# Sparse chunk attention and a routed expert layer on one core: token layout by pairs of tiles, one PSUM bank per head, one gather row, later constants

## The chip, the cores and the metric

One core of a Trainium2 chip runs the whole program in one launch. The metric is device time in microseconds. Of the kernel before there are two runs, 395.28 and 399.24 us, median 397.26; a further execution was profiled. The engines are named as in the profile: PE (TensorE), PEld (its weight loads), DVE (VectorE), ACT (ScalarE), POOL (GpSimd) and SP (SyncE, which here only issues transfers).

## What is computed

Attention with 4 batches, 8 heads, 768 positions and 64 features. For each query an upper bound on its score with each chunk of 32 keys is formed from the chunk's smallest and largest key; the six best causal chunks are kept, and softmax attention runs over their causal keys alone. The result, as 3072 tokens of 512 features, goes through a dense layer pair for all tokens plus one of eight experts for each.

```python
k_min = np.min(k_chunks, axis=3); k_max = np.max(k_chunks, axis=3)
ub = sum(maximum(q * k_min, q * k_max), axis=-1)      # by query and chunk
ub = where(causal, ub, -1e9); top_chunks = argsort(ub)[..., -6:]
scores = scale * q @ k.T, kept where the chunk is in top_chunks and pos_q >= pos_k
attn = softmax(scores) @ v
x = attn.transpose(0, 2, 1, 3).reshape(3072, 512)
y = relu(x @ w1_dense) @ w2_dense
e = argmax(x @ w_gate);  gate = max(softmax(x @ w_gate))
y += gate * (relu(x @ w1[e]) @ w2[e])                  # each token's own expert
```

## The kernel before

**Attention** goes over 16 pairs of heads (`NP`), four to a batch. A tile is 128 consecutive tokens; a head has six (`NT`). For a pair p, `load` (L257) issues six transfers of 192 KB from SP, one for each of k, q, v and each head, in runs of one token's 64 floats (256 bytes). `cast` (L265) makes 16-bit copies on POOL. `prep_k` (L273) transposes k on PE, reduces it on DVE to chunk maxima and minima (L280, L281) and copies it to `kT` beside rows that carry the chunk mask (`exf`). `prep_q` (L288) transposes q, `prep_ub` (L298) forms the bounds by small products on top of the causal constant `cbias`, takes the eight largest of 24 by `max` (L311) and writes where a chunk is out (L313) into spare columns of `q16`; tile 0 is left out, since its queries see at most four chunks. `prep_s` (L316) transposes those columns with q, so one product gives masked scores.

The scores come in units of up to 512 columns (`PIECES`, L130): key tile bb against query tiles from bb on, 11 units a pair with both heads interleaved. `scores` (L324) is one or more products (L330), an exponential on ACT (L334) and, on the diagonal tile, a select on POOL (L344, `affine_select`) that clears later keys. `av` (L348) multiplies with v into `op`, one PSUM tile of two banks for both heads (L362), and `norm` (L366) divides at the end of the pair (L370, L371) into `xbig`.

The loop (L391) starts the scores two units ahead. At each pair's first unit it issues the loads of pair p + 3 (three load buffers), one expert weight on POOL (`load_expert`, 1 MB of floats, L126) and the casts of p + 2. After each batch the dense work of its tokens is queued as `fills`: transposes (L181), the gate (L189), two dense layers (L217, L226) and writes of x to `xd` (L206) and of the dense y to `yd` (L231). A planner of the framework orders each engine's instructions by its own cost estimates, so an instruction without dependences, such as a weight load, can stand earlier than in the text.

**Start.** Constants are made on POOL and DVE ahead of everything (L53 to L112); loads of pairs 0, 1 and 2, then `load_dense` and the casts follow.

**Routing** (L449 to L509): after the last batch's gate, token positions in expert-sorted blocks of 128 are computed on DVE and PE (31 blocks, `NBLK`); `gi` and `si` hold the gather and scatter rows.

**Expert blocks** (L590 on): `gather` fetches 128 rows of `xd` (1,056 bytes, L523) and 128 rows of `yd` (2,048 bytes, L526) from POOL's queue; `tx` transposes x (L533, copied at L535), `e1` is the first product (L541, ACT at L544), `th` transposes (L550, L552), `e2` the second (L558), the weighted sum `yo` with y on DVE (L561) and a scatter from POOL (L562). The tiles of x, y and yo have three buffers each (`eg`), and gathers run two blocks ahead.

## Time and profile before

| | |
|---|---|
| two runs, median | 397.26 us (395.28 to 399.24) |
| profiled execution | 394.51 us |
| its span, first to last instruction | 392.8 us |
| busy: PE, PEld | 258.8, 152.8 us |
| busy: DVE, ACT, POOL | 192.1, 159.7, 208.0 us |
| moved by DMA | 56.92 MB in 98,370 packets, of them 78,462 under 512 B |
| mean granted clock of PE | 0.907 of full |

Busy times overlap; a share over the whole span mixes three stages: attention to 213 us, routing to some 240 us, expert blocks to the end. In the slices each digit is the busy share in tenths of one fortieth of the span. A wait names who waited, for whom, and how long in all, how often, and the longest. Times in rows are microseconds from the start of the span; "mean ns" is one instruction's.

### The profile page before, as it was taken

The page shows a single profiled execution, that of the slowest core. Times are in us where ns is not written, and L with a number is a line of the kernel's source. Part 1 is how long each engine was busy: PE and PEld are TensorE (multiplying, and loading weights), DVE is VectorE, ACT ScalarE, POOL GpSimd, SP SyncE. Part 2 cuts the span into 40 slices and gives each one's busy share as a digit, 9 for nine tenths or more (in the row PEclk, how much of TensorE's full clock was granted, in tenths as well). Part 3 has the DMA queues.
Part 4 walks back from the last instruction along what each step waited for, and adds up shares of the span by engine and source line. Part 5 has one row for each costly group of instructions (what it writes and reads, how often), then busy time and mean ns, then how long its engine had stood idle before and what let it go on. Part 6 is the DMA issues. An engine that isn't in the chain of part 4 may idle for free. (4 is left out here: it accounts for less than half of the span.)

```text
span 392.8 us, 7052 instructions
## 1 busy us (share of the span) xinstructions
PE 258.8 (66%) x2426; PEld 152.8 (39%) x2426; DVE 192.1 (49%) x538; ACT 159.7 (41%) x303; POOL 208.0 (53%) x370
## 2 busy tenths in 40 slices
PE   0157377157599989999898872667555658565660
PEld 0135254045365666666665531333222323222230
DVE  8284438248387798777952890222222323232220
ACT  1016257056276867787675320322132222322230
POOL 9946185174455555554322025366756656666541
PEclk9998869779699999999999996888989996989895
DMA  9999999999997886211031425143444444444440
GB/s 182 208 222 214 208 204 198 170 199 204 222 236 191 190 200 145 94 53 56 3 119 49 164 106 173 42 154 114 131 133 132 149 145 135 134 136 133 128 121 0
DMA packets 98370, 56.92 MB, mean 145 GB/s; under 512 B 78462, under 2 KB 90750, under 8 KB 98336
## 3 DMA queue, kind: packets, MB, share of 16 engines
q1 hardware_dynamic: 81856, 28.42, 32.8%
q0 software_dynamic: 16480, 28.06, 30.1%
q8 instruction: 20, 0.33, 0.3%
q14 instruction: 14, 0.11, 0.1%
HBM read 50.08 MB, written 17.66 MB: 172 GB/s over the span
## 5 line engine op out<-in xcount | busy, mean ns | idle before, releaser
L334 ACT ACTIVATE ex<-sp 128x512 f16<-128x512 f32 (+1 forms) x176 | 91.7, 585 | 63.1 <-PE sp L330 31.1
L344 POOL TENSOR_SCALAR_AFFINE_SELECT ex<-ex 128x128 f16<-128x128 f16 (+1 forms) x176 | 52.2, 306 | 55.9 <-ACT ex L334 53.0
L362 PE MATMUL op<-v,ex 128*128 128x65 f16 x672 | 47.6, 200 | 34.6 <-POOL ex L344 29.7
L330 PE MATMUL sp<-r,kT 128*128 128x512 f16 (+3 forms) x256 | 65.1, 328 | 3.6 <-ACT ex L334 2.1
L362 PEld LDWEIGHTS <-ex 128*128 128x128 f16 x672 | 37.3, 101 | 49.5 <-POOL ex L344 35.0
L535 DVE COPY exT<-tp 128x512 f16<-128x512 f16 x31 | 13.2, 425 | 80.5 <-PE tp L533 59.3
L523 POOL DMA_INDIRECT xg<-xd,gi x31 | 30.3, 977 | 41.5 <-DVE yo L561 21.6
L552 ACT COPY ehT<-tp 128x512 f16<-128x512 f16 x31 | 18.2, 586 | 74.2 <-PE tp L550 67.9
L541 PE MATMUL hp<-we,exT 128*128 x124 | 37.4, 432 | 10.2 <-DVE exT L535 5.8
L558 PE MATMUL yp<-we,ehT 128*128 x124 | 38.8, 419 | 4.5 <-ACT ehT L552 2.6
L533 PE MATMUL tp<-ident,xg 128*128 128x128 f16 x124 | 14.2, 247 | 40.7 <-DMA xg<-xd,gi 40.7
L562 POOL DMA_INDIRECT out_dram<-yo,si x31 | 31.5, 1015 | 15.3 <-issue 13.4
L561 DVE SCALAR_TENSOR_TENSOR yo<-yp,xg,yg 128x512 f32<-128x512 f32 x31 | 23.3, 750 | 31.9 <-PE yp L558 27.2
L526 POOL DMA_INDIRECT yg<-yd,gi x31 | 29.4, 949 | 10.5 <-issue 10.2
L322 DVE COPY r<-pp 128x768 f16<-128x768 f16 x32 | 17.0, 554 | 32.8 <-PE pp L320 32.6
L544 ACT ACTIVATE eh<-hp 128x512 f16<-128x512 f32 x31 | 18.5, 597 | 35.2 <-PE hp L541 26.3
L533 PEld LDWEIGHTS <-xg 128*128 128x128 f16 x124 | 8.3, 108 | 56.9 <-DMA xg<-xd,gi 56.8
L217 PE MATMUL hp<-xT,wd 128*128 128x384 f16 x128 | 26.5, 325 | 0.7 <-ACT hT L219 0.3
L330 PEld LDWEIGHTS <-kT 128*128 128x128 f16 x256 | 21.8, 103 | 11.1 <-issue 8.2
L226 PE MATMUL yp<-wd,hT 128*128 128x512 f16 x96 | 24.6, 378 | 1.5 <-DVE xbig L371 1.0
L269 POOL CAST q<-qf 128x768 f16<-128x768 f32 x16 | 13.3, 831 | 21.5 <-DMA qf<-in_q_dram 20.9
L294 ACT ACTIVATE qp<-pp 128x768 f16<-128x768 f16 x16 | 13.0, 810 | 23.1 <-PE pp L292 23.1
(115 smaller groups left out, 431.0 us busy)
## 6 DMA issues: line engine op xcount, KB each, us to landing
we<-in_moe_w_dram POOLq DMA_DIRECT2D x16, 512.0 KB
kf<-in_k_dram SPq DMA_DIRECT2D x32, 192.0 KB, 4.4
qf<-in_q_dram SPq DMA_DIRECT2D x32, 192.0 KB, 4.5
vf<-in_v_dram SPq DMA_DIRECT2D x32, 192.0 KB, 4.7
yd<-ys SPq DMA_DIRECT2D x24, 256.0 KB, 2.1
xd<-xbig SPq DMA_DIRECT2D x4, 792.0 KB, 4.3
wd<-in_moe_w_dense_dram POOLq DMA_DIRECT2D x2, 512.0 KB
xg<-xd,gi POOLq DMA_INDIRECT x31
```

What stands on the lines that cost most here:

```text
L217: nc.tensor.matmul(hp, wd[:, ko, j * 128 : (j + 1) * 128], xT[:, ko, g * G * 128 : (g + 1) * G * 128], start=(ko == 0), stop=(ko == NK - 1))
L226: nc.tensor.matmul(yp, hold["h"][:, j, i * 128 : (i + 1) * 128], wd[:, NK + j], start=(j == 0), stop=(j == NK - 1))
L330: nc.tensor.matmul(sp[:, o : o + z - a], kT[p % NB][g][:, bb * 128 : (bb + 1) * 128], s["r", g][:, a:z], start=(o == 0), stop=True, skip_g ...
L334: nc.scalar.activation(ex[:, :o], sp[:, :o], AF.Exp, scale=0.125)
L344: nc.gpsimd.affine_select(out=exd, in_=exd, compare_op=ALU.is_ge, fill=0.0, base=0, pattern=[[0, n], [1, 128]], channel_multiplier=-1)
L362: nc.tensor.matmul(op[:, g, t * (D + 1) : (t + 1) * (D + 1)], ex[:, c : c + 128], v16[p % NB][:, g, bb, :], start=(u == g and n == 0), sto ...
L523: nc.gpsimd.indirect_dma_start(out=xg, out_offset=None, in_=xd, in_offset=bass.IndirectOffsetOnAxis(ap=gi[:, i : i + 1], axis=0))
L526: nc.gpsimd.indirect_dma_start(out=yg, out_offset=None, in_=yd, in_offset=bass.IndirectOffsetOnAxis(ap=gi[:, i : i + 1], axis=0))
L541: nc.tensor.matmul(hp, s["xT"][:, ko], wef[:, bass.ds(offs[i] + ko * 512, 512)], start=(ko == 0), stop=(ko == NK - 1))
L558: nc.tensor.matmul(yp, s["hT"][:, j], wef[:, bass.ds(offs[i] + (NK + j) * 512, 512)], start=(j == 0), stop=(j == NK - 1))
L561: nc.vector.scalar_tensor_tensor(o, yp, s["x"][:, Dm : Dm + 2].bitcast(FP), s["y"], ALU.mult, ALU.add)
L562: nc.gpsimd.indirect_dma_start(out=out, out_offset=bass.IndirectOffsetOnAxis(ap=si[:, i : i + 1], axis=0), in_=o, in_offset=None, bounds_c ...
```

## The change

Attention tiles now come in pairs. Of 256 consecutive tokens partition p holds tokens 2p and 2p + 1, the first in tile 2T, the second in tile 2T + 1. One run of a load is then two tokens, 512 bytes. Both key tiles of a pair meet both query tiles of it, so the units become 12 of 512 columns for each pair of heads, one head after the other; selects cover 256 or 512 columns with a pattern in three dimensions; bounds and maxima cover tile 0 too; chunk reductions go by three groups of 256 columns. `op` is one bank for each head, with two buffers, and `norm` runs for each head. x and the dense y share a DRAM row (`xd`, 3,104 bytes), with one gather of it and four buffers, three blocks ahead. Scatters are declared independent of each other. Loads of pairs 0 and 1 are issued ahead of all constants; the constants that POOL makes for attention follow the first casts, `load_dense` and the routing constants move into pairs 1 and 2, memsets move to DVE, and one routing product (L484) takes its factor as a tensor.

```diff
+    RW = 2 * Dm + XW
...
-    xd = dram.tile([N, XW], U16, name="xd")
-    yd = dram.tile([N, Dm], FP, name="yd")
+    xd = dram.tile([N, RW], U16, name="xd")
+    xdv = xd.rearrange("(T p j) w -> p T j w", p=128, j=2)
...
+    NJ = 2
+    NT2 = NT // NJ
...
+    def load(p):
+        b, hp = divmod(p, HP)
+        for nm, src in (("k", k), ("q", q), ("v", v)):
+            f = aload.tile([128, 2, NT, D], FP, name=nm + "f")
+            st[p][nm] = f
+            for g in range(2):
+                nc.sync.dma_start(out=f[:, g].rearrange("p (T j) d -> p T (j d)", j=NJ),
+                                  in_=src[b, 2 * hp + g].rearrange("(T p j) d -> p T (j d)", p=128, j=NJ))
+    load(0)
+    load(1)
...
-        nc.gpsimd.memset(q16[i], 0.0)
-        nc.gpsimd.memset(v16[i][:, :, :, D : D + 1], 1.0)
+        nc.vector.memset(q16[i][:, :, 0:64], 0.0)
+        nc.vector.memset(q16[i][:, :, 192:256], 0.0)
...
+    exf = acst.tile([32, S], HF)
+    nc.vector.memset(exf, -30000.0)
+    def consts():
+        for g in range(2):
+            nc.gpsimd.affine_select(out=cbias[:, :, g, :], in_=cbias[:, :, g, :], compare_op=ALU.is_ge,
+                                    fill=-60000.0, base=0, pattern=[[256, NT2], [1, NJ], [-32, NC]], channel_multiplier=2)
+        pat = [[256, NT2], [1, NJ], [2, 128]]
+        npat = [[-a, n] for a, n in pat]
+        nc.gpsimd.affine_select(out=exf, in_=exf, compare_op=ALU.is_ge, fill=0.0,
+                                base=0, pattern=pat, channel_multiplier=-32)
+        nc.gpsimd.affine_select(out=exf, in_=exf, compare_op=ALU.is_ge, fill=0.0,
+                                base=31, pattern=npat, channel_multiplier=32)
+        for i in range(NB):
+            for g in range(2):
+                r0 = 64 * g
+                nc.vector.memset(kT[i][g][r0 : r0 + 64], 0.0)
+                nc.vector.tensor_copy(kT[i][g][r0 : r0 + 32, :], exf)
...
+    def route_consts():
+        nc.gpsimd.memset(xbig[:, :, Dm:XW], 0.0)
+        nc.gpsimd.iota(iom8, pattern=[[0, NT], [1, E]], base=-E, channel_multiplier=0, allow_small_or_imprecise_dtypes=True)
...
     PIECES = [
         [(0, 0, 512)],
-        [(1, 128, 640)],
-        [(0, 512, 768), (4, 512, 768)],
+        [(1, 0, 512)],
+        [(0, 512, 768), (1, 512, 768)],
         [(2, 256, 768)],
-        [(1, 640, 768), (3, 384, 768)],
+        [(3, 256, 768)],
+        [(4, 512, 768), (5, 512, 768)],
     ]
-    units = []
-    for pc in PIECES:
-        for g in range(2):
-            units.append([(g,) + x for x in pc])
-    units.append([(g, 5, 640, 768) for g in range(2)])
-    first_of = {}
+    units = [(g, pc) for g in range(2) for pc in PIECES]
+    NU = len(units)
...
-            nc.sync.dma_start(out=xd[b * S : (b + 1) * S].rearrange("(m p) w -> p m w", p=128),
-                              in_=xbig[:, b * NT : (b + 1) * NT].bitcast(U16))
+            for j in range(NJ):
+                nc.sync.dma_start(out=xdv[:, b * NT2 : (b + 1) * NT2, j, 2 * Dm :],
+                                  in_=xbig[:, b * NT + j : (b + 1) * NT : NJ].bitcast(U16))
...
-                nc.sync.dma_start(out=yd[m * 128 : (m + 1) * 128], in_=ys)
+                nc.sync.dma_start(out=xdv[:, m // NJ, m % NJ, 0 : 2 * Dm], in_=ys.bitcast(U16))
...
-        tc.tile_pool(name="pout", bufs=1, space=bass.MemoryType.PSUM) as pout,
+        tc.tile_pool(name="pout", bufs=2, space=bass.MemoryType.PSUM) as pout,
...
-            pkc = pk.rearrange("d (c w) -> d c w", w=32)
-            nc.vector.tensor_reduce(out=ks[:, 0, :], in_=pkc, op=ALU.max, axis=mybir.AxisListType.X)
-            nc.vector.tensor_reduce(out=ks[:, 1, :], in_=pkc, op=ALU.min, axis=mybir.AxisListType.X)
+            for T in range(NT2):
+                pkc = pk[:, T * 256 : (T + 1) * 256].rearrange("d (j c w) -> d c j w", j=NJ, w=16)
+                kc = slice(T * 8, T * 8 + 8)
+                nc.vector.tensor_reduce(out=ks[:, 0, kc], in_=pkc, op=ALU.max, axis=mybir.AxisListType.XY)
+                nc.vector.tensor_reduce(out=ks[:, 1, kc], in_=pkc, op=ALU.min, axis=mybir.AxisListType.XY)
...
+            g, pc = units[u]
             sp = psc.tile([128, 512], FP, name="sp")
             o = 0
-            for g, bb, a, z in un:
-                nc.tensor.matmul(sp[:, o : o + z - a], kT[p % NB][g][:, bb * 128 : (bb + 1) * 128],
+            for kt, a, z in pc:
+                nc.tensor.matmul(sp[:, o : o + z - a], kT[p % NB][g][:, kt * 128 : (kt + 1) * 128],
                                  s["r", g][:, a:z], start=(o == 0), stop=True, skip_group_check=True)
                 o += z - a
             ex = aexp.tile([128, 512], HF, name="ex")
-            nc.scalar.activation(ex[:, :o], sp[:, :o], AF.Exp, scale=0.125)
-            o = 0
-            dg = []
-            for g, bb, a, z in un:
-                if a == bb * 128:
-                    dg.append(o)
-                o += z - a
-            if dg:
-                n = len(dg)
-                exd = ex[:, dg[0] : dg[0] + n * 128]
-                nc.gpsimd.affine_select(out=exd, in_=exd, compare_op=ALU.is_ge, fill=0.0, base=0,
-                                        pattern=[[0, n], [1, 128]], channel_multiplier=-1)
+            nc.scalar.activation(ex, sp, AF.Exp, scale=0.125)
...
+            n = sum(a == (kt // NJ) * 256 for kt, a, z in pc)
+            if n:
+                exd = ex[:, 0 : n * 256]
+                nc.gpsimd.affine_select(out=exd, in_=exd, compare_op=ALU.is_ge, fill=0.0, base=-(pc[0][0] % NJ),
+                                        pattern=[[-1, n], [1, NJ], [2, 128]], channel_multiplier=-2)
...
+            first = u % len(PIECES) == 0
+            if first:
+                s["op", g] = pout.tile([128, 512], FP, name="op")
+            op = s["op", g]
...
+        def norm(p, g):
             b, hp = divmod(p, HP)
-            opv = st[p]["op"][:, :, : NT * (D + 1)].rearrange("p g (t e) -> p g t e", e=D + 1)
-            rs = ahead.tile([128, 2, NT, 1], FP, name="rs")
-            nc.vector.reciprocal(rs, opv[:, :, :, D : D + 1])
-            nc.vector.tensor_tensor(
-                xbig[:, b * NT : (b + 1) * NT, hp * 128 : (hp + 1) * 128].rearrange("p t (g d) -> p g t d", g=2),
-                opv[:, :, :, 0:D], rs.to_broadcast([128, 2, NT, D]), ALU.mult)
+            opv = st[p]["op", g][:, : NT * (D + 1)].rearrange("p (t e) -> p t e", e=D + 1)
+            rs = ahead.tile([128, NT, 1], FP, name="rs")
+            nc.vector.reciprocal(rs, opv[:, :, D : D + 1])
+            h0 = (2 * hp + g) * D
+            nc.vector.tensor_tensor(xbig[:, b * NT : (b + 1) * NT, h0 : h0 + D],
+                                    opv[:, :, 0:D], rs.to_broadcast([128, NT, D]), ALU.mult)
...
-        load(0)
-        load(1)
-        load(2)
-        load_dense()
         cast(0)
-        cast(1)
+        consts()
         prep_k(0)
         prep_q(0)
         prep_ub(0)
+        prep_s(0, 0)
+        prep_s(0, 1)
+        load(2)
+        cast(1)
         prep_k(1)
         prep_q(1)
-        prep_s(0, 0)
-        prep_s(0, 1)
...
+                if p == 1:
+                    load_dense()
+                if p == 2:
+                    route_consts()
...
+            if u == NU // 2 - 1:
+                norm(p, 0)
             if u == NU - 1:
-                norm(p)
+                norm(p, 1)
...
-        tc.tile_pool(name="eg", bufs=3) as eg,
+        tc.tile_pool(name="eg", bufs=4) as eg,
...
-        nc.vector.tensor_scalar(Bm[:, :, 1, :], eqb, iop, None, ALU.mult)
+        nc.vector.tensor_tensor(Bm[:, :, 1, :], eqb, iop.unsqueeze(2).to_broadcast([128, NM, NBLK]), ALU.mult)
...
-            s["x"] = xg = eg.tile([128, XW], U16, name="xg")
+            s["x"] = xg = eg.tile([128, RW], U16, name="xg")
             nc.gpsimd.indirect_dma_start(out=xg, out_offset=None, in_=xd,
-                                         in_offset=bass.IndirectOffsetOnAxis(ap=gi[:, i : i + 1], axis=0))
-            s["y"] = yg = eg.tile([128, Dm], FP, name="yg")
-            nc.gpsimd.indirect_dma_start(out=yg, out_offset=None, in_=yd,
...
+            if i:
+                tc.declare_no_dep(sc.ins, group="scatter", reason="each scatter writes rows of its own")
+            tc.add_to_no_dep_group("scatter", sc.ins)
...
+        gather(2)
         tx(0)
         for i in range(NBLK):
             e1(i)
-            if i + 2 < NBLK:
-                gather(i + 2)
+            if i + 3 < NBLK:
+                gather(i + 3)
```

## Rows read from the trace of the kernel before

**Rows 1.** The page's slices of the span, the DMA engines' busy share.

```profile
DMA  9999999999997886211031425143444444444440
```

**Rows 2.** The waits of 16 to 106 us.

```profile
PEld L362 <- POOL ex L344: 32.0, 12, 9.5
...
POOL q L269 <- DMA qf<-in_q_dram: 20.9, 4, 7.6
```

**Rows 3.** DMA view: queues of 16 to 106 us, GB/s slices of 214 to 240 us.

```profile
q0 software_dynamic: 9864, 9.44, 64.0%
q1 hardware_dynamic: 35099, 8.81, 52.5%
...
GB/s 0 0 0 359 167 369 315 0 0 0 0 0 247 359 349 289 16 0 325 372 88 16 25 6 0 0 0 0 54 369 378 6 0 22 362 110 205 315 175 195
```

**Rows 4.** Timeline of DVE: normalisations of pairs 0, 1, 2, 4 and 15 (start, duration).

```profile
45.09 0.96 DVE L371 TENSOR_TENSOR xbig<-op,rs 128x768 f16<-128x768 f32 x1
...
60.82 0.96 DVE L371 TENSOR_TENSOR xbig<-op,rs 128x768 f16<-128x768 f32 x1
...
69.29 0.96 DVE L371 TENSOR_TENSOR xbig<-op,rs 128x768 f16<-128x768 f32 x1
...
105.78 0.95 DVE L371 TENSOR_TENSOR xbig<-op,rs 128x768 f16<-128x768 f32 x1
...
212.48 0.96 DVE L371 TENSOR_TENSOR xbig<-op,rs 128x768 f16<-128x768 f32 x1
```

**Rows 5.** Window 115.3 to 204.9: PE, PEld, DVE, ACT, POOL busy (count), clock, DMA, GB/s.

```profile
115.30:204.90 89.60, 83.01 (x1040) 55.31 (x1037) 71.36 (x225) 65.57 (x132) 43.89 (x116) 1.00 0.48 121
```

**Rows 6.** Timeline of the start (POOL, PE); from the DMA issues, k's landing time.

```profile
15.56 0.87 POOL L268 CAST k<-kf 128x768 f16<-128x768 f32 x1
...
28.18 0.58 PE L330 MATMUL sp<-r,kT 128*128 128x512 f16 x1
...
kf<-in_k_dram SPq DMA_DIRECT2D x32, 192.0 KB, 4.4
```

**Rows 7.** Groups by form: busy us and mean ns of one, then idle time before them.

```profile
L362 PE MATMUL op<-v,ex 128*128 128x65 f16 x672 | 47.6, 200 | 34.6 <-POOL ex L344 29.7 <-DVE xbig L371 3.0 <-ACT ex L334 1.0
L344 POOL TENSOR_SCALAR_AFFINE_SELECT ex<-ex 128x128 f16<-128x128 f16 x160 | 45.8, 295 | 51.4 <-ACT ex L334 49.2 <-DMA kf<-in_k_dram 1.0 <-DMA vf<-in_v_dram 0.2
...
L330 PE MATMUL sp<-r,kT 128*128 128x512 f16 x96 | 36.5, 408 | 1.9 <-ACT ex L334 1.4
...
L280 DVE TENSOR_REDUCE ks<-pp 128x24 f16<-128x768 f16 x16 | 15.3, 953 | 12.4 <-PE pp L277 12.2
...
L344 POOL TENSOR_SCALAR_AFFINE_SELECT ex<-ex 128x256 f16<-128x256 f16 x16 | 6.5, 409 | 4.5 <-ACT ex L334 3.8 <-DMA kf<-in_k_dram 0.7
```

**Rows 8.** The waits of 244 to 384 us, PE's for the gather.

```profile
PEld L533 <- DMA xg<-xd,gi: 51.9, 28, 3.1
```

**Rows 9.** Timeline of the expert blocks: PE's first and last L541, two POOL rows.

```profile
243.92 3.57 PE L541 MATMUL hp<-we,exT 128*128 x8 [3.26 <-issue]
...
302.35 0.95 POOL L526 DMA_INDIRECT yg<-yd,gi  x1 [0.30 <-issue]
...
306.51 0.98 POOL L523 DMA_INDIRECT xg<-xd,gi  x1 [1.89 <-DVE yo L561]
...
378.94 1.02 PE L541 MATMUL hp<-we,exT 128*128 x4
```

**Rows 10.** Timeline: first gather, last y write, last but one scatter.

```profile
235.14 1.06 POOL L523 DMA_INDIRECT xg<-xd,gi  x1 [6.20 <-PE yp L226]
236.00 0.32 SPq L231 DMA_DIRECT2D yd<-ys  x1
...
383.51 0.98 POOL L562 DMA_INDIRECT out_dram<-yo,si  x1 [1.86 <-DMA out_dram<-yo,si]
```

**Rows 11.** Timeline of the start: POOL's selects on the causal constant, a DVE copy.

```profile
3.82 1.74 POOL L67 TENSOR_SCALAR_AFFINE_SELECT cbias<-cbias 128x144 f16<-128x144 f16 x2
3.88 1.49 DVE L83 COPY kT<-exf 32x768 f16<-32x768 f16 x1 [0.51 <-POOL exf L61]
```

More of the change, by code (lines that the diff above doesn't have):

```diff
@@ L308, in prep_ub @@
             m8 = ahead.tile([128, NT, 2, 8], FP, name="m8")
-            for t in range(1, NT):
+            for t in range(NT):
                 for g in range(2):
@@ L411 @@
                 prep_s(n1, 0)
-            if u == 5 and n1 is not None:
+            if u == 6 and n1 is not None:
                 prep_s(n1, 1)
@@ L415 @@
                 prep_k(n2)
-            if u == 8 and n2 is not None:
+            if u == 9 and n2 is not None:
                 prep_q(n2)
@@ L427 @@
             load_expert(*wq.pop(0))
+    att.close()
     with (
```

124 lines of the change are left out of this document (50 added, 74 removed).

## The prediction

> **What bounds the kernel now.** I read the page's slices first, then the waits, DMA view and timeline of each stage, because no engine is the limit throughout. There are three stages.
>
> *Attention to about 106 us* is bound by transfers. The DMA slices stand at 9 until 130 us [rows 1]. The waits of 16 to 106 us show how it reaches the compute: POOL's cast of q waits 20.9 us for its load, and since POOL works in order, the selects behind that cast wait too; TensorE's weight load of the value product then waits 32.0 us for them [rows 2]. q1 (q, k, v) and q0 (weights) share the engines there: q1 moves 8.81 MB in 52.5% of 90 us, 47.3 us of sixteen engines or 186 GB/s, q0 moves 9.44 MB in 57.6 us [rows 3]. The five pairs 0 to 4 end at 45.1, 60.8, 69.3, then 89.2, and 105.8 us [rows 4]; the pair that ends at 69.3 took 8.5 us, which is what one costs when nothing is late and no dense work is mixed in.
>
> *Attention from 106 to 213 us* is TensorE's: 83.0 of 89.6 us busy at granted clock 1.00 (2.4 GHz), DVE 71.4, ACT 65.6, POOL 43.9 [rows 5]. Eleven pairs in 212.5 - 105.8 = 106.7 us are 9.7 us each, dense layers included [rows 4].
>
> *The expert blocks* take (378.94 - 243.92) / 30 = 4.50 us each [rows 9]. TensorE's first load of a block waits 51.9 us in all for the gather of x [rows 8]; that gather in turn waits for the buffer that the weighted sum yo three blocks earlier gives back (idle 1.89 us before the one at 306.51) [rows 9]. So the end is set by a loop of three blocks: yo, gather, landing, two matrix products, yo, about 13.5 us.
>
> **The change, part by part.**
>
> *Start.* The first cast begins at 15.56 us, behind all constants and the dense weights' issue; first scores at 28.18 [rows 6]. A k load lands some 4.4 us after its issue [rows 6], so with loads first the cast can begin near 5 us. From cast to scores took 12.6 us; the second pair's preparation leaves this stretch (about 4 of it), while the select constants enter on POOL behind the first casts. I put first scores at 15 us, bounds 12 (all constants hidden) and 22 (none).
>
> *Loads.* The 96 loads of 192 KB take 36,864 packets in place of 73,728. No row has 512-byte runs. The nearest are 256 bytes at 186 GB/s [rows 3], 22 ns a packet on each of sixteen engines, and 2 KB writes, whose slices reach 359 to 378 GB/s [rows 3], 91 ns. A straight line between these gives 12 ns a packet and 0.0385 ns a byte, so 32 ns for 512 bytes: 257 GB/s, which I take; the bounds are 186 and 360. A pair's 1.18 MB then costs 4.6 us of all engines in place of 6.3; with q1's share of 52.5% that is 8.8 us per pair, below the 9.6 that the compute is going to take. Then casts are hardly late, and the next late thing is the compute itself.
>
> A packet rule speaks against that much. The Trainium skill, "DMA: Bandwidth & Descriptors", section "Why small descriptors are slow (HBM only)", says that a packet pays some 3 cycles beside one cycle per 32 bytes. By it 512 bytes cost 19 cycles for two times 11, only 14% less, as an estimate from that page; the time would be that of the third case below.
>
> *More work per pair, since a key tile now meets both query tiles of its pair.* TensorE: scores 3072 columns a head for 2688, so 768 more a pair, 1.5 products of 512 at 36.5/96 = 0.38 us, 0.57 us; value products 48 for 42 at 47.6/672 = 0.07, 0.42 us [rows 7]. Together 1.0 us, all on the path in the TensorE-bound stretch; some of it lies in pipelined ends, I take 0.9. ACT: 12 exponentials for 11; even if all its 73% were these, it would reach 80%. DVE: reductions 6 for 2 (2 x 0.95 become 6 at 0.95/3 plus a start, 2.1 to 2.5 us) [rows 7], two more maxima and a second normalisation, under 1 us of 9.7 at 80% busy: beside TensorE, though close to it. POOL selects: before, ten at 0.295 and one at 0.409; now eight of 256 at 0.409 and two of 512, extrapolated by 0.114 per 128 columns to 0.64: 4.55 for 3.36 us, +1.2 us at half-busy POOL [rows 5, 7]: hidden. The pattern of the select has one more dimension; its price is bounded in the last case below.
>
> *A bank for each head.* The next product no longer waits for the whole pair's normalisation; under 1 us a pair, which I count as the cover for DVE's added work.
>
> *Sum of attention.* First scores 15; pair 0 takes 10 (it took 16.9 with late loads); pairs 1 to 3 at 8.5 + 1.1 = 9.6; twelve pairs at 9.7 + 0.9 = 10.6. 15 + 10 + 28.8 + 127.2 = 181, plus 5 for loads still late while weights run: 186 for 213.4, a gain of 27.4 us. Bounds: 177 (no late load, start at 12) and 206 (loads as dear as now).
>
> *Queues moved past.* load_dense and the routing constants move to pairs 1 and 2 on POOL, into time when POOL waited; SP gets two x writes for one in each batch, 0.4 us each, behind loads issued three pairs ahead. If POOL has no such gaps, their 5 us come once.
>
> *Routing.* x and y share rows, so the first gather must wait for the last y write as well. Before, it went at 235.14 us, and the last y write was issued only at 236.00 [rows 10]; its landing takes about 1.9 us more, judged by the wait for a scatter's landing [rows 10]. Behind that gather on POOL stand only the other gathers; TensorE waits for them. +3 us, of which 1 is covered because the first product waited 3.26 us on issue after its data [rows 9]: +2, bounds 0 and 5.
>
> *Expert blocks.* One gather instruction less: 0.95 + 0.30 us [rows 9]. POOL's own line becomes two instructions, 2.6 us a block where it was 3.9. The landing has 2 KB x 128 more in it, 262 KB at 360 GB/s, +0.7 us. With four buffers the loop covers four blocks: (13.5 - 1.25 + 0.7) / 4 = 3.2 us. Thirty times 4.5 - 3.2 is 39 us. Bounds: 2.6 (POOL alone) and 3.9 (no help from the fourth buffer beyond POOL's). Scatters no longer wait for each other; before, the last but one waited 1.86 us [rows 10]; -2 us at the end.
>
> *Sum:* 392.8 - 27.4 + 2 - 39 - 2 = 326.4 us span. The profiled execution took 394.5 us, 1.7 more than its span, and the median of the runs (397.3) lies 2.75 above it: 326.4 + 1.7 + 2.75 = **331 us**.
>
> **The forecast and its rivals.**
>
> 1. *As forecast, 331 us.* Chance 0.42.
>
> 2. *Loads stay the limit.* If 512 bytes cost as much per byte as 256 do, pairs 1 to 4 keep their pace of (105.8 - 45.1) / 4 = 15.2 us [rows 4] instead of 9.6 and 10.6: 3 x 5.6 + 4.6 = 21, of which the 5 us already counted for late loads are part, but the preparation of later pairs comes late too; I put it at 20: 351 us. For it: both queues were saturated [rows 3]. Against: 2 KB writes run at twice the rate. Chance 0.12.
>
> 3. *Loads gain a seventh.* If most of a packet's time goes by its bytes, the same pairs come every 13.1 us: 3 x 3.5 + 2.5 = 13, so 344 us. For it: nothing between 256 bytes and 2 KB was measured. Against: the straight line above. Chance 0.10. This is what the page's rule would make.
>
> 4. *The expert loop does not shorten.* The larger row lands later and the block order on TensorE keeps a product behind each late gather; 3.87 us a block, 331 + 20 = 351. For it: yo still stood right before the gather that TensorE needed next [rows 9]. Against: one more buffer puts a whole block between. Chance 0.15; together with case 2 (371 us) 0.05.
>
> 5. *Better:* blocks at POOL's 2.6 us (-18) and loads never late (-7): 306 us. Chance 0.12.
>
> 6. *Slower: the selects.* POOL's select on a two-dimensional pattern of 144 elements took 0.87 us (two in 1.74) [rows 11], 6 ns an element against 1.6 for the 256-wide form [rows 7]. If the new three-dimensional pattern costs that, the ten selects take 8 x 1.55 + 2 x 3.1 = 19 us a pair, 22 with casts, and attention ends at 25 + 15 x 22 = 355: 331 + 169 = 500 us. It decides from 1.24 us a select: then a pair is POOL's 15.7 us, attention ends at 260, and the time is 405. Against: the operand itself stays contiguous with an inner run of 128, as in the 0.3 us form, and that slow pair ran beside a DVE copy of 1.49 us [rows 11]. Chance 0.04.
>
> The Trainium skill, "SBUF — State Buffer", section "Who interferes with whom", says that POOL and a DVE copy between SBUF tiles lock each other out of one shared port pair. The trace agrees as far as it goes: copies of this form took 1.49 us beside that select [rows 11]. By that rule the 0.87 us would be waiting and not work, and case 6 would fall.
>
> **How the numbers follow.** The chances are those above. About two per cent is what a measurement of this kernel can tell from no change. Every case but the sixth lies well under 389 us, so faster has 0.95, the same 0.01, slower 0.04. The range runs from 306, the better case, to 365, past cases 2 to 4; outside lie half of case 5, most of 2 and 4 together, and case 6.
>
> **What would show it.** Right: q1 with 36,864 fewer packets; the DMA slices below 9 before 110 us; no wait of POOL's casts above 3 us; first scores near 15, last normalisation near 186; blocks at 3.2 us and TensorE's wait for xg under 20 us in all; selects at 0.41 and 0.64. Wrong: normalisations before 90 us still 13 us or more apart (case 2), gathers still idle for yo and TensorE for them (case 4), selects over 1 us (case 6), DVE over 95% busy in the pairs with dense work, in which case it, not TensorE, sets them.

## The result and the profile after

The kernel after takes 342.99 us, median of two runs (341.96 to 344.02), for 397.26 before: 0.863 of the time, 95% interval 0.842 to 0.885. The forecast of 331 us was 12 us low; the range held. The profiled execution has a span of 340.3 us for 392.8.

The page's slices of DMA's busy share, as in [rows 1]:

```profile
DMA  7999999999999834512003122226165766566550
```

The nines still run to slice 13, some 110 us. The waits of 20 to 103 us, to be laid beside [rows 2]:

```profile
PEld L376 <- POOL ex L356: 21.0, 26, 8.0
...
POOL q L284 <- DMA qf<-in_q_dram: 7.3, 2, 7.0
```

TensorE waits 21.0 us for selects where it waited 32.0, and the cast of q 7.3 us for its load where it waited 20.9. Fewer, but not gone. The queues of 40 to 90 us (packets, MB, share of sixteen engines' time; in this stretch q0 carries the weights, q1 the loads):

```profile
q0 software_dynamic: 6948, 6.90, 81.3%
q1 hardware_dynamic: 8348, 4.11, 38.0%
```

The same 50 us of the kernel before:

```profile
q0 software_dynamic: 5349, 5.31, 64.1%
q1 hardware_dynamic: 17715, 4.44, 49.1%
```

Over 16 to 88 us, until pair 4 ends in the kernel after and with no writes yet in the loads' queue, the kernel after and then the kernel before:

```profile
q0 software_dynamic: 8919, 8.35, 69.5%
q1 hardware_dynamic: 16887, 8.30, 48.9%
```

```profile
q0 software_dynamic: 8574, 8.17, 69.5%
q1 hardware_dynamic: 25074, 6.29, 48.2%
```

Here nearly the same weights go beside the loads, and the loads' share of the engines is as before; 8.30 MB in 48.9% of 72 us are 236 GB/s of their own time, for 181. In 40 to 90 us more weights go beside them than before; the share is 38.0% for 49.1%, the rate 216 GB/s for 181. (The two queues' shares together pass 100%, so packets of both are timed at once.) Over the whole run the loads' queue has 45,056 packets for 81,856: 36,800 fewer. The ends of pairs 0, 3, 4 and 15, as in [rows 4] (each pair now has two such rows; these are the second):

```profile
42.36 0.55 DVE L386 TENSOR_TENSOR xbig<-op,rs 128x384 f16<-128x384 f32 x1
...
68.66 0.55 DVE L386 TENSOR_TENSOR xbig<-op,rs 128x384 f16<-128x384 f32 x1
...
87.79 0.54 DVE L386 TENSOR_TENSOR xbig<-op,rs 128x384 f16<-128x384 f32 x1
...
202.05 0.56 DVE L386 TENSOR_TENSOR xbig<-op,rs 128x384 f16<-128x384 f32 x1
```

Pair 0 ends at 42.4; pairs 1 to 3 take 8.8 us each, pair 4 takes 19.1, and the other eleven 10.39. The start, against [rows 6]:

```profile
1.38 0.95 POOL L162 DMA_DIRECT2D we<-in_moe_w_dram  x1 [0.37 <-issue]
...
11.80 0.83 POOL L284 CAST q<-qf 128x768 f16<-128x768 f32 x1 [6.76 <-DMA qf<-in_q_dram]
...
16.89 5.38 DVE L120 COPY kT<-exf 32x768 f16<-32x768 f16 x6 [7.66 <-POOL exf L114]
...
27.93 0.63 PE L347 MATMUL sp<-r,kT 128*128 128x512 f16 x1
```

First scores come at 27.93, hardly earlier than before (28.18). Ahead of the casts POOL issues an expert weight at 1.38 us; the cast of q then waits 6.76 us for its load; the selects of the constants stand behind the casts, and DVE waits 7.66 us for them before it can copy `exf` into `kT`. The groups by form, against [rows 7]:

```profile
L356 POOL TENSOR_SCALAR_AFFINE_SELECT ex<-ex 128x256 f16<-128x256 f16 x128 | 51.0, 407 | 37.4 <-ACT ex L351 33.8 <-DMA qf<-in_q_dram 1.3
...
L356 POOL TENSOR_SCALAR_AFFINE_SELECT ex<-ex 128x512 f16<-128x512 f16 x32 | 20.4, 639 | 9.2 <-ACT ex L351 8.5
```

The selects cost 407 and 639 ns, where 409 and 640 were foreseen. The expert stage, against [rows 8] and [rows 9]: the waits of 230 to 330 us, then the first gather, the first and last `e1`, and the last scatter.

```profile
PEld L549 <- DMA xg<-xd,gi: 30.2, 22, 8.1
...
POOL xg L542 <- DVE yo L577: 26.1, 16, 10.5
```

```profile
228.06 1.07 POOL L542 DMA_INDIRECT xg<-xd,gi  x1 [10.88 <-DMA xd<-ys]
...
236.74 1.86 PE L557 MATMUL hp<-we,exT 128*128 x4 [4.02 <-issue]
...
331.13 1.08 PE L557 MATMUL hp<-we,exT 128*128 x4 [0.16 <-DVE exT L551]
...
336.27 0.98 POOL L578 DMA_INDIRECT out_dram<-yo,si  x1 [1.14 <-DVE yo L577]
```

A block takes (331.13 - 236.74) / 30 = 3.15 us for 4.50. POOL's gather still waits for `yo`. The first gather waits 10.88 us for the dense y rows.

Stage by stage, measured against forecast: attention ends at 202.6 for 186 (+16.6); from there to the first `e1` 34.1 us for 32.5 (+1.6); thirty blocks 94.4 for 96 (-1.6); the tail 9.2 for 11.9 (-2.7). The miss lies in attention. Inside it, pair 0 ends 17.4 us later than the 25 foreseen, pairs 1 to 3 are 2.5 us quicker, and the rest is 1.7 dearer, the 5 us for late loads included.

### The profile page after: what moved, and what is told of

The parts are those of the page before. It is cut to its first block, busy times and chain, and to the rows that moved or that the text cites. A ratio compares the mean times of both kernels' runs of the same rounds, so it can differ in the third digit from the quotient of the medians.

```text
span 340.3 us, 7383 instructions
## 1 busy us (share of the span) xinstructions
PE 253.5 (75%) x2554; PEld 152.4 (45%) x2554; DVE 205.1 (60%) x680; ACT 171.2 (50%) x319; POOL 191.3 (56%) x312
## 3 DMA queue, kind: packets, MB, share of 16 engines
q1 hardware_dynamic: 45056, 28.42, 29.3%
HBM read 50.08 MB, written 17.66 MB: 199 GB/s over the span
## 4 chain that ended last, share of the span: by engine, by line
POOL 24%; issue 22%; PE 22%; DMA 14%; DVE 10%; ACT 6%; SPq 1%; POOLq 1%; ACTq 0%; DVEq 0%
POOL out_dram L578 9%; PE yp L252 5%; POOL ex L356 5%; DMA qf<-in_q_dram 5%; DMA kf<-in_k_dram 5%; PE sp L347 4%; POOL xg L542 4%; PE hp L243 4%; ACT ex L351 4%; PE op L376 3%; DMA vf<-in_v_dram 3%; PE pp L337 2%; DVE kT L120 2%; POOL k L283 1%; DVE Am L515 1%
## 5 line engine op out<-in xcount | busy, mean ns | idle before, releaser
L351 ACT ACTIVATE ex<-sp 128x512 f16<-128x512 f32 x192 | 103.7, 617 | 47.8 <-PE sp L347 41.8
L356 POOL TENSOR_SCALAR_AFFINE_SELECT ex<-ex 128x256 f16<-128x256 f16 (+1 forms) x160 | 70.5, 453 | 46.6 <-ACT ex L351 42.3
L376 PE MATMUL op<-v,ex 128*128 128x65 f16 x768 | 57.9, 196 | 20.3 <-POOL ex L356 17.2
L347 PE MATMUL sp<-r,kT 128*128 128x512 f16 (+1 forms) x256 | 70.6, 331 | 1.1 <-ACT ex L351 0.4
L376 PEld LDWEIGHTS <-ex 128*128 128x128 f16 x768 | 41.8, 98 | 47.3 <-POOL ex L356 30.8
L557 PE MATMUL hp<-we,exT 128*128 x124 | 33.5, 391 | 8.2 <-issue 5.5
L549 PE MATMUL tp<-ident,xg 128*128 128x128 f16 x124 | 12.7, 227 | 19.7 <-DMA xg<-xd,gi 19.4
L577 DVE SCALAR_TENSOR_TENSOR yo<-yp,xg 128x512 f32<-128x512 f32 x31 | 23.2, 747 | 5.6 <-PE yp L574 3.7
L328 DVE MAX8 m<-pp 128x8 f32<-128x24 f32 x192 | 18.9, 176 | 12.3 <-PE pp L322 12.2
L245 ACT ACTIVATE hT<-hp 128x384 f16<-128x384 f32 x32 | 15.9, 498 | 13.5 <-PE hp L243 6.8
L297 DVE TENSOR_REDUCE ks<-pp 128x8 f16<-128x256 f16 x48 | 20.0, 417 | 1.9 <-PE pp L292 1.3
```

The costliest lines, as they stand in the source:

```text
L347: nc.tensor.matmul(sp[:, o : o + z - a], kT[p % NB][g][:, kt * 128 : (kt + 1) * 128], s["r", g][:, a:z], start=(o == 0), stop=True, skip_g ...
L351: nc.scalar.activation(ex, sp, AF.Exp, scale=0.125)
L356: nc.gpsimd.affine_select(out=exd, in_=exd, compare_op=ALU.is_ge, fill=0.0, base=-(pc[0][0] % NJ), pattern=[[-1, n], [1, NJ], [2, 128]], c ...
L376: nc.tensor.matmul(op[:, t * (D + 1) : (t + 1) * (D + 1)], ex[:, c : c + 128], v16[p % NB][:, g, kt, :], start=(first and n == 0), stop=(l ...
L549: nc.tensor.transpose(tp[:, ko], s["x"][:, 2 * Dm + ko * 128 : 2 * Dm + (ko + 1) * 128].bitcast(HF), ident)
L557: nc.tensor.matmul(hp, s["xT"][:, ko], wef[:, bass.ds(offs[i] + ko * 512, 512)], start=(ko == 0), stop=(ko == NK - 1))
```

## The experiments

The runs were made in groups of one to four on one chip, the kernel before beside them; it took 393 to 399 us, so ratios to it compare better than times. In runs that leave the code of the expert stage as it is, a block takes 3.00 to 3.25 us (3.15 in the kernel after), so 0.2 us a block are not read as an effect. Unless the text says on what it builds, a run differs from the kernel after only by its diff. Ends of attention are the last normalisation's start plus its 0.56 us.

### The start: constants and the first weight

**Constants first.**

```diff
+        consts()
         cast(0)
-        consts()
```

> Only the order of the first casts and the attention constants on POOL is turned round; the first expert weight is still issued before the casts. In the changed kernel q's first cast waits 6.8 us for its load, the constant exf is ready at 16.9 us, and first scores come at 27.9 us; span 340.3. Theory order (constants behind the casts hold DVE, which works in order): exf is ready by 8 us, DVE's copies run while q is awaited, first scores come near 19 us, span near 331. Theory transfer (the early weight makes q late, and all else follows q): q still lands near 11.8 us, first scores move by 3 us at most, span 337 to 341.

Measured: 348.96 us, ratio 0.875 (0.871 to 0.880). First scores come at 19.31 us for 27.93, so the constants do hold the start up by 8.6 us. None of it reaches the end: attention ends at 206.3. In 20 to 110 us the cast of q now waits longer (7.3 us in the kernel after):

```profile
POOL q L284 <- DMA qf<-in_q_dram: 12.4, 3, 6.8
```

**Weights behind the casts of pair 1.** `vc` is pair 1's cast of v; all experts and, in the same way, the dense weights are put behind it.

```diff
-                    load_expert(*wq.pop(0))
+                    with tc.issue_after(st[1]["vc"].ins):
+                        load_expert(*wq.pop(0))
```

> Only the weights are held back: no weight is issued before the casts of pair 1. Theory transfer: q lands by 6 us and v by 7 instead of 11.8 and 13, everything behind them on POOL moves with them, first scores near 22, span near 334. Theory order says the same 6 us are to be had only as far as the constants move with the casts, so first scores between 20 and 23 too; what tells it apart is the sum: with both theories true the kernel with both edits gains as much as the two alone. Rival (the loads' own pace makes q late, not the weight): q still lands after 10 us and nothing moves.

Measured: 344.97 us, ratio 0.867 (0.862 to 0.871). q is cast at 6.11 us for 11.80, first scores at 23.94, pair 0 ends at 39.3, yet pair 4 at 87.2 and attention at 201.9.

**Both edits.**

> Constants first and weights held back. Both theories true: first scores near 14 us, as forecast for the change itself, span near 326 to 328 if nothing later takes it back; if the weights, now later, lengthen the stall of pair 4 (19.1 us for 10.6), up to 5 us of it are given back. Only one true: 19 to 22 us for first scores, span 331 to 335.

Measured: 345.03 us, ratio 0.867 (0.861 to 0.872). First scores come at 19.68 us, no earlier than with the constants first alone (19.31): once the constants are out of the way, the weight does not hold the first scores. Pair 0 ends at 34.3, 8 us earlier than in the kernel after; pair 4 at 85.1, attention at 203.2. Three kernels with three starts, and pair 4 ends at 85 to 92 us in each. The start was not the limit; something fills up until then.

### The weights: when they are issued

**One expert weight for each pair.** On top of both edits, each expert weight stands behind the cast of v of the pair after its own; the program makes that cast during the pair before.

```diff
+                    with tc.issue_after(st[min(p + 1, NP - 1)]["vc"].ins):
+                        load_expert(*wq.pop(0))
```

> As the run with both edits, and each expert weight is issued only after the casts of the pair before its own, one weight a pair over the whole attention. Theory bunching (weights issued together share the DMA engines with q, k, v between 30 and 92 us and make the casts of pair 6 late, which costs pair 4 some 8.5 us): pair 4 takes 10 to 11 us, no cast waits over 2 us for a load, span 8 us below the run with both edits, near 318. Rival (512-byte loads are too slow by themselves): pair 4 stays above 15 us. Rival (TensorE and DVE take it back, since a pair then always carries dense work or a weight): span within 3 us of the run with both edits.

Measured: 334.16 us, ratio 0.839 (0.835 to 0.844). Pair 4 takes 11.4 us, near the 10 to 11 of the theory, but the span is 331.6 us for some 318 expected. Pair 4 ends at 78.8 and attention at 193.6. Pair 1 now takes 16.5 us: both dense weights and two experts still went out between 12.7 and 19.8 us.

**All weights paced.** With the constants first, each weight is put behind a select of its own pair, none before 32 us. `load_dense` is here the gate and the first dense matrix, `load_dense2` the second.

```diff
+            if u in (2, 8):
+                with tc.issue_after(st[p]["sel"].ins):
+                    if u == 2 and p == 1:
+                        load_dense()
+                    elif u == 2 and p == 2:
+                        load_dense2()
+                    elif p >= 13 or u == 2 and p >= 3:
+                        load_expert(*wq.pop(0))
```

> Constants first, and every weight transfer issued behind a named select of its pair: the gate and the first dense matrix in pair 1, the second in pair 2, one expert half in each of pairs 3 to 12, two in each of 13 to 15, none beside the first loads. The work is the same. Theory that the bunching of weights in the first 90 us was the attention stage's loss: first scores at 18 to 20 us, pair 0 ends at 33, pairs 1 to 3 at 8.5 to 9.5 each, pair 4 at 68 to 72 us (87.8 as changed, 78.8 with the first pacing), later pairs 10.4; attention ends at 182 to 190 us and the time is 321 to 330. Rival, by which a pair's loads plus any one weight beside them cost more than the pair's compute (4.6 us of loads and about 6 us of weights against 8.8 to 10.4): the stalls only move to later pairs, attention ends at 193 to 203 us and the time stays at 332 to 343.

Measured: 320.27 us, ratio 0.815 (0.812 to 0.819). The same transfers and the same arithmetic, in another order. Its start, the ends of pairs 4 and 15, two of POOL's weight issues and, from 30 to 85 us, the queues:

```profile
18.48 0.63 PE L349 MATMUL sp<-r,kT 128*128 128x512 f16 x1
...
50.04 0.76 POOL L164 DMA_DIRECT2D we<-in_moe_w_dram  x1
...
58.70 0.76 POOL L164 DMA_DIRECT2D we<-in_moe_w_dram  x1
...
69.91 0.54 DVE L388 TENSOR_TENSOR xbig<-op,rs 128x384 f16<-128x384 f32 x1
...
183.31 0.56 DVE L388 TENSOR_TENSOR xbig<-op,rs 128x384 f16<-128x384 f32 x1
```

```profile
q1 hardware_dynamic: 14965, 7.84, 49.2%
q0 software_dynamic: 3632, 3.09, 41.6%
...
qf<-in_q_dram SPq DMA_DIRECT2D x10, 192.0 KB, 3.9
```

The same rows of the kernel after (the last number is a load's median time from issue to landing):

```profile
q0 software_dynamic: 7345, 7.30, 78.1%
q1 hardware_dynamic: 10306, 5.07, 41.0%
...
qf<-in_q_dram SPq DMA_DIRECT2D x10, 192.0 KB, 12.7
```

With 3.09 MB of weights beside it in place of 7.30, the loads' queue moves 7.84 MB (1.6 of them already writes of x and y) in place of 5.07 in that time, and a load of q lands in 3.9 us in place of 12.7. Pair 4 ends at 69.9 for 87.8, attention at 183.9 for 202.6. In the kernel after, 12 of the 16 expert weights are issued by 62 us, because the planner puts an instruction that waits for nothing wherever POOL has a gap; in this run two are. Against the run with both edits, which starts as early, attention ends 19.3 us sooner: the bunch was the loss. Of the 18.7 us against the kernel after, 10.3 lie before the end of pair 0 (32.0 for 42.4), where the run with both edits had won 8 and lost them again, and 7.9 in pair 4 (11.2 for 19.1).

### The parts of the change

**256-byte runs again**, in the new layout: each load is split by the two tokens.

```diff
+                for j in range(NJ):
+                    nc.sync.dma_start(out=f[:, g, j:NT:NJ],
+                                      in_=src[b, 2 * hp + g].rearrange("(T p j) d -> p T j d", p=128, j=NJ)[:, :, j])
```

> The layout of the change is kept, each load of q, k, v is split by the two tokens of a pair, so that it goes in 256-byte runs again (twice the DMAs on SP, twice the packets; nothing else is touched). Theory that the 512-byte runs carry the attention stage's gain: packets of the loads' queue go back by 36,864 (45,056 to about 81,900); the loads are again what ends last, so early pairs with weights beside them cost 12 to 15 us each instead of 9 to 10, attention ends at 215 to 225 us for 202.6, and the time is 353 to 368 us. Rival, by which the two PSUM banks or the pairs of tiles carry the gain and the runs are beside the point: attention ends at 200 to 206 us and the time stays at 340 to 346.

Measured: 362.69 us, ratio 0.918 (0.909 to 0.926); 83,456 packets; attention ends at 225.8, just past the 215 to 225 of the theory, and pairs 1 to 4 take (111.72 - 46.68) / 4 = 16.3 us each. The window of 8 to 16 us, in which the loads are nearly alone, in this kernel and in the kernel after:

```profile
q1 hardware_dynamic: 6514, 1.60, 91.0%
```

```profile
q1 hardware_dynamic: 4090, 2.01, 87.9%
```

1.60 MB in 7.28 us of sixteen engines is 220 GB/s; 2.01 MB in 7.03 us is 286. So 512-byte runs are 1.30 times as fast here; the forecast had 257 / 186 = 1.38 times. The rule of the Trainium skill, "DMA: Bandwidth & Descriptors", section "Why small descriptors are slow (HBM only)", makes that 1.16 times (an estimate from its cycles: 22 for 19). These two windows do not agree with it, and beside equal weights, in 16 to 88 us of the kernels before and after, the step is 1.30 times as well (181 to 236 GB/s).

**One bank.**

```diff
-        tc.tile_pool(name="pout", bufs=2, space=bass.MemoryType.PSUM) as pout,
+        tc.tile_pool(name="pout", bufs=1, space=bass.MemoryType.PSUM) as pout,
```

> The two PSUM banks in which the heads' products are summed in turn become one; all else as changed. Theory: each head's first value product then waits for the head before to be normalised (reciprocal and 0.56 us sum, with DVE's queue ahead of it, some 1 us a head as in the kernel before, where the wait for xbig was 29.7 us in all over 16 pairs), partly covered: 32 heads by 0.5 to 1 us, attention ends at 216 to 235 us for 202.6, time 355 to 375. Rival, by which the products of scores and preparation fill the gap on TensorE and the bank is beside the point: attention ends at 200 to 207 us, time 340 to 347.

Measured: 352.27 us, ratio 0.898 (0.895 to 0.901); attention ends at 213.6, where the runs with the kernel after's attention stage ended it at 202.6 to 205.9. That is between the two expectations. Pairs 5 to 15 take (213.03 - 93.55) / 11 = 10.86 us for 10.39, so the second bank is worth 0.5 us a pair there. The rest is a pair 4 that ends at 93.6, for 87.8 to 91.8 in those runs; why is open.

**Three buffers in the expert blocks.**

```diff
-        tc.tile_pool(name="eg", bufs=4) as eg,
+        tc.tile_pool(name="eg", bufs=3) as eg,
...
-            if i + 3 < NBLK:
-                gather(i + 3)
+            if i + 2 < NBLK:
+                gather(i + 2)
```

> The pool of gathered rows has three buffers for four, and the gather runs two blocks ahead for three; the single gather stays. Theory that the fourth buffer sets the block's period (a buffer is taken at the gather's issue and given back by the residual sum some 12.6 us later: 12.6/4 = 3.15): the block costs 4.0 to 4.4 us and the time is 368 to 380 us, with GpSimd's gather waiting for the residual sum and its row not back to back. Rival, by which GpSimd's two issues (0.98 + 0.98 us and gaps) set the period: 3.1 to 3.3 us, time within 340 to 347.

Measured: 389.87 us, ratio 0.988 (0.981 to 0.994): nearly the whole gain of the change is gone. In the profiled execution, at the upper end of its times, a block takes (382.26 - 240.60) / 30 = 4.72 us, more than either theory gave, and more than the 4.50 of the kernel before. If all 3.7 us by which that execution passes the median lay in its blocks, it would still be 4.6 (an estimate). Its window of 300 to 320 us, and that of the kernel after (PE, PEld, DVE, ACT, POOL busy with counts, granted clock, DMA share, GB/s):

```profile
300.00:320.00 20.00, 12.49 (x62) 5.61 (x59) 4.71 (x8) 4.74 (x8) 8.54 (x9) 0.83 0.43 128
```

```profile
300.00:320.00 20.00, 15.21 (x96) 7.23 (x96) 6.78 (x12) 7.09 (x12) 12.36 (x14) 1.00 0.62 203
```

The gather lands 4.0 us after its issue, which is 1.2 more than the 2.8 of the x rows alone (below); and TensorE, busy 12.49 us of 20 for 15.21, has a mean granted clock of 0.83 for 1.00 (2.4 GHz).

**Scatters in order.** The declaration that they are independent is taken out.

```diff
-            if i:
-                tc.declare_no_dep(sc.ins, group="scatter", reason="each scatter writes rows of its own")
-            tc.add_to_no_dep_group("scatter", sc.ins)
```

> The declaration that the scatters need no order among themselves is taken out, as in the kernel before; all else as changed. Theory: the scatter's issue waits for the one before it to land (about 2 us after its issue), which lies beside 3.15 us of a block and costs nothing there, while the tail gets back 0 to 2 us: time 342 to 346. Rival, by which the order held each block up because GpSimd waits in order and the next gather stands behind it: 3.6 to 4.5 us a block, time 355 to 385.

Measured: 358.82 us, ratio 0.910 (0.903 to 0.917). Blocks take 3.25 us, within the spread of the same code elsewhere, so they hardly feel it. But each scatter waits for the landing of the one before, falls behind, and four are still to be issued when the last sum begins:

```profile
338.05 1.02 PE L557 MATMUL hp<-we,exT 128*128 x4 [0.38 <-DVE exT L551]
...
343.92 0.75 DVE L577 SCALAR_TENSOR_TENSOR yo<-yp,xg 128x512 f32<-128x512 f32 x1 [2.29 <-DMA out_dram<-yo,si]
...
353.67 0.98 POOL L578 DMA_INDIRECT out_dram<-yo,si  x1 [1.85 <-DMA out_dram<-yo,si]
```

From the last `e1` to the end it is 19.6 us for 9.2. Both theories were wrong on the place.

**Two gathers**, from a tensor each, with four buffers.

```diff
+            nc.gpsimd.indirect_dma_start(out=xg, out_offset=None, in_=xd,
+                                         in_offset=bass.IndirectOffsetOnAxis(ap=gi[:, i : i + 1], axis=0))
+            s["y"] = yg = eg.tile([128, Dm], FP, name="yg")
+            nc.gpsimd.indirect_dma_start(out=yg, out_offset=None, in_=yd,
+                                         in_offset=bass.IndirectOffsetOnAxis(ap=gi[:, i : i + 1], axis=0))
```

> Two tensors and two gathers for each block again, as before (row of 1,040 bytes and row of 2,048 bytes), with four buffers and the same three blocks ahead; no order among scatters. Theory that GpSimd's issues bound the block: three indirect DMAs of 0.98 us plus gaps give 3.6 to 4.0 us, time 352 to 368, GpSimd busy over 2.9 us of each. Rival, by which the buffers alone bound it and the single row is beside the point: 3.1 to 3.3 us, time 338 to 346 (the first gather may start some 3 us earlier, since the x rows are written before the dense rows).

Measured: 359.76 us, ratio 0.913 (0.907 to 0.919). A block takes (346.06 - 233.46) / 30 = 3.75 us with POOL's row back to back, three issues each 0.30 us behind the last:

```profile
267.56 0.97 POOL L544 DMA_INDIRECT xg<-xd,gi  x1 [0.30 <-DVE exT L556]
268.84 0.95 POOL L547 DMA_INDIRECT yg<-yd,gi  x1 [0.30 <-issue]
270.09 1.03 POOL L583 DMA_INDIRECT out_dram<-yo,si  x1 [0.30 <-issue]
```

The gather of x, rows of 1,056 bytes (not the 1,040 of the expectation), lands in 2.8 us here. The first one goes at 224.25 us where the two kernels above it, with the single row, go at 231.9, because it need not wait for the y rows.

### Further, from these readings

**Offsets and early x.** On top of the paced weights: TensorE reads the blocks' offsets behind its last dense product (`cur["last"]`), and the x rows also go to a tensor of their own, from which blocks 0 and 1 take x.

```diff
+        with tc.issue_after(cur["last"].ins):
+            lds, offs = nc.values_load_multi_w_load_instructions(
...
+            if i < 2:
+                s["e"] = xe = et.tile([128, XW], U16, name="xe")
+                nc.gpsimd.indirect_dma_start(out=xe, out_offset=None, in_=xs,
+                                             in_offset=bass.IndirectOffsetOnAxis(ap=gi[:, i : i + 1], axis=0))
```

> As the run before it, and two more: TensorE reads the blocks' offsets into registers right behind its last dense product, while the first gather is under way, instead of between the first block's weight load and its product; and the x rows are written to a tensor of their own as well (768 KB more written in all), from which the first two blocks take x without waiting for the dense rows (GpSimd issues two more gathers). Theory: the wait on issue ahead of the first expert product (4.0 us) goes, and the first gather goes 5 to 7 us earlier, of which 3 to 6 reach the end: together 6 to 9 us less than the run with the paced weights alone. Rival, by which the first blocks then wait for the full rows anyway (their y part, three gathers later on GpSimd): 3 to 4 us less, the offsets alone.

Measured: 312.74 us, ratio 0.796 (0.793 to 0.799). First `e1` at 211.42 for 218.64 in the run with paced weights, and without the wait on issue:

```profile
211.42 1.88 PE L577 MATMUL hp<-we,exT 128*128 x4
```

The first gather goes at 206.59 us for 210.07. How much of the 7.2 us each of the two edits gave was not tried apart. (The second copy of the x rows adds 3.2 MB of writes in all, not 768 KB: the loads' and writes' queue moves 31.66 MB for 28.42.)

**Five buffers**, on top of that.

```diff
-        tc.tile_pool(name="eg", bufs=4) as eg,
+        tc.tile_pool(name="eg", bufs=5) as eg,
...
+                gather(i + 4)
```

> As the run with offsets and early x rows, but the gathered rows and their sums have five buffers for four and the gather runs four blocks ahead for three; nothing else. Theory that the loop from a buffer's gather to its return still sets the block's period (3.03 us by four is 12.1): by five that is 2.4, so GpSimd's two instructions with their gaps become the bound, 0.97 + 1.02 + 2 x 0.30 = 2.6 us a block, and the time falls by 29 blocks x 0.4 = 11 to 13 us, to 299 to 303. Rival, by which the block is held by the order of products on TensorE and its own chain (transposition, copy, product, Relu, transposition, copy, product), or by the gather's landing and not by the buffer: 2.95 to 3.1 us, the time stays at 311 to 314.

Measured: 300.83 us, ratio 0.763 (0.759 to 0.766), the fastest here. A block takes (291.05 - 211.69) / 30 = 2.65 us, and POOL issues without a gap:

```profile
250.41 0.98 POOL L561 DMA_INDIRECT xg<-xd,gi  x1 [0.30 <-issue]
251.69 1.02 POOL L598 DMA_INDIRECT out_dram<-yo,si  x1 [0.30 <-issue]
253.02 0.98 POOL L561 DMA_INDIRECT xg<-xd,gi  x1 [0.30 <-issue]
```

A row of 0.98, one of 1.02 and two gaps of 0.30 make the block. With four buffers it was the loop, with five it is POOL.

## Why the prediction came out as it did

**The start: wrong, and the largest miss.** "I put first scores at 15 us, bounds 12 (all constants hidden) and 22 (none)"; 27.93 was measured, outside both bounds. The step took the constants off the path because they follow the casts, but POOL works in order: the selects that DVE and the scores need now stood behind casts that wait for transfers. It also counted only what was written ahead of the casts; the weight that the planner put there (1.38 us) was not in it. Turning the two round and holding the weights back gives 19.68, and 18.48 with all weights paced. That is still over 15: from the first cast (4.45 us there) to scores it takes 14 us, not 10.

**Loads: the rate nearly right, the share wrong where it counted.** 257 GB/s was foreseen; 236 was measured beside the weights of 16 to 88 us, 286 with the loads nearly alone. What failed is "with q1's share of 52.5% that is 8.8 us per pair": an average over 90 us of the kernel before was carried to every pair, while the weights were issued closer together. At the 236 GB/s and 48.9% of 16 to 88 us 1.18 MB would come to 10.2 us, at the 216 GB/s and 38.0% of 40 to 90 us they come to 14. Pairs 0 to 2 had been cast by 21.7 us, so the price fell on pair 4, in the kernel after:

```profile
70.94 0.82 POOL L284 CAST q<-qf 128x768 f16<-128x768 f32 x1 [6.98 <-DMA qf<-in_q_dram]
```

POOL stands 6.98 us at the cast of a later pair's q, and pair 4's selects stand behind it. The sign "the DMA slices below 9 before 110 us" did not come. The prediction had also misread it in the kernel before: the nines of [rows 1] end after twelve slices of 9.8 us, at 118 us and not at 130.

**Late loads and the start were one term, not two.** The sum had 5 us for loads still late, and a start 13 us earlier beside it. The first three runs show that an earlier start only lengthens the later wait: pair 4 ends at 85 to 92 us whatever the start, until the weights are moved. With them moved and the constants first, attention ends at 183.9, against 186 foreseen: the compute terms of the sum were right, and the order of the start and of the transfers made the 18.7 us to the 202.6 of the kernel after.

**Compute per pair: right.** 10.39 us for 10.6, selects at 407 and 639 ns, and 8.8 for 9.6 in the pairs without dense work. From 97.6 to 202.0 us TensorE is busy 98.1 of 104.4 us and DVE 80.1, so TensorE still sets the pace and DVE is far from the sign's 95%. Case 6 (selects at 6 ns an element) is out, and its source was misread: the 0.87 us of [rows 11] is the mean of two unlike selects. The first line below has both in the kernel before (shortest, middle, longest in ns), the second the same two, by then with the three-dimensional pattern, in the kernel after:

```profile
L67 POOL TENSOR_SCALAR_AFFINE_SELECT cbias<-cbias x2: 332/890/1448, 3.8 to 4.1; 128x144 f16<-128x144 f16 x2
...
13.79 0.65 POOL L108 TENSOR_SCALAR_AFFINE_SELECT cbias<-cbias 128x144 f16<-128x144 f16 x2
```

The long one of 1.45 us ran beside DVE's copy of 1.49; without a copy beside them the two take 0.65 us together, 2.3 ns an element. The prediction had put the slow row down to a lock with DVE's copy by the Trainium skill, "SBUF — State Buffer", section "Who interferes with whom"; the trace agrees, as far as these prices go. The second bank was put at "under 1 us a pair"; the run without it shows 0.5.

**Routing: right in kind.** +2 us foreseen, +3.6 found (34.1 for 30.5 from attention's end to the first `e1`). Where the x rows do not wait for the y rows, the first gather goes 7.7 us earlier.

**Expert blocks: right.** 3.15 us for 3.2, by the loop over four buffers. The lower bound was read well: with five buffers 2.65 (on top of the paced weights), against the 2.6 given for POOL alone. The upper was not: without the fourth buffer a block takes 4.72, against the 3.9 of the bound and the 4.3 that the prediction's loop gives by three; what fills the rest is open. One term was mis-sized: the larger row lands 1.2 us later, not 0.7. TensorE's wait for the gather is 30.2 us, not under 20 as the prediction's sign had it; 8.1 of that is the first gather, and with the loop at the buffers' bound some wait stays in every block. So the sign of case 4, gathers idle for yo and TensorE for them, came without case 4 and could not tell the two apart.

**Scatters: right sign, too small.** "-2 us at the end" was 4.7 between the two kernels (13.9 to 9.2), and without the declaration the quicker blocks would have cost 10.4 at the end.

**The cases.** The time of 343 us is that of case 3 (344), but not by its course: it had pairs 1 to 4 at 13.1 us each by a lower rate; three of the four took 8.8, and only pair 4, with 19.1, showed the sign of case 2 (13 us or more before 90 us); and the rate was higher than even the forecast's where the loads were nearly alone (286 for 257). The range held because it was drawn past cases 2 to 4; the start lay outside its own bounds, and late loads were given 5 us.

## What to carry to other kernels

A queue's average share over a long stretch does not say what one step inside it gets. A term for "what is late next" has to be made from the order in which transfers are issued, and that order belongs to the planner wherever an instruction waits for nothing: read it, and tie prefetches to the work that they may run beside. Two gains that end in the same queue are not added; ask where the second would wait. In a pipelined loop write down both prices, the loop divided by its buffers and the issuing engine's row, and see which is larger after the change, not before.

## What the runs showed that was not expected

- 512-byte runs go 1.30 times as fast as 256-byte runs both where the loads are nearly alone (286 and 220 GB/s) and beside equal weights (236 and 181). Fewer packets did not cost the loads their share of the engines: beside 8.35 and 8.17 MB of weights it was 48.9% with 16,887 packets and 48.2% with 25,074. It fell to 38.0% where the weights were bunched.
- A weight is counted in the queues by the 512 KB that it writes, but it is read as 1 MB of floats: only so do loads, weights and gathers add up to the page's 50.08 MB of HBM reads. By that the kernel after reads 4.11 + 2 x 6.90 = 17.9 MB in 40 to 90 us, 358 GB/s, for 301 in the kernel before (estimates from the queues' rows). A bunch of weights asks for twice the reads that the queue's bytes suggest; that these reads were the limit is not shown.
- The three parts of the expert stage do not add up: without the fourth buffer, the single gather or the scatters' freedom the ratio is 0.988, 0.913 and 0.910 for 0.863, together more than the whole stage gained.
- Loops that leave TensorE waiting also came with a lower mean granted clock over the blocks: 0.84 with three buffers, 0.90 in the kernel before, 0.94 with two gathers, 0.98 in the kernel after. That this is why three buffers cost more than four thirds of 3.15 us, or 4.2, is not shown.
- In the kernel after the wait on issue ahead of the first expert product is 4.02 us; the program's order has the read of 31 offsets into TensorE's registers there, and behind the last dense product it shows no wait.
